# One attention unit's last products, kept keys and last queries rearranged in a fused attention and two-layer kernel

## Chip, cores and metric

The kernel runs on one core of a Trainium2 chip. Times are device microseconds of one launch. In the texts TensorE is PE in the rows, VectorE DVE, ScalarE ACT, GpSimd POOL, and SP the engine that issues the DMAs.

## What is computed

Sliding-window attention with a linear bias over 4 batches, 8 heads, 576 positions and 64 dimensions, followed by two feed-forward layers over the 2304 rows of 512:

```python
scores = scale * np.matmul(q, k.transpose(0, 1, 3, 2))
bias = slopes[:, None, None] * (-np.abs(rel).astype(np.float32))[None, :, :]
mask = (rel >= 0) & (rel < 128)
scores = np.where(mask, scores + bias[None], -1000000000.0)
...                                   # softmax over the keys
x = np.matmul(attn, v)                # then (tokens, 512)
h = np.maximum(x @ w_in, 0.0)
x = (h * h) @ w_out                   # 512 -> 2048 -> 512
x = 1 / (1 + np.exp(-(x @ w_gate))) * (x @ w_val) @ w_out2   # 512 -> 1536 -> 512
```

All is float32; the layers' operands are split into a high and a low part, three matmuls for each product.

## The kernel before

A query sees the 128 keys up to its own, so 128 queries need two key tiles of 128, their own and the one before. A **unit** is the attention of one batch for one pair of heads: kind a holds queries 0 to 255, kind b 256 to 511; kind c holds the last 64 queries of all four head pairs at once. Eight **chunks** of tokens are worked through in order: a and b of batch 0, a and b of batch 1 (four units each), then a with c of batch 0, b with c of batch 1, and so on (five units each). The first layer of a chunk (`h_step` and `y_step`, lines 795 to 861, 16 steps of each) runs while the units of the next chunk are worked on between its matmuls; the layers of chunks 0 and 1 are interleaved. The second layer (line 873 on) starts when all eight chunks are done.

A group of two head pairs is **turned** once (`turn`, line 558): queries (`nq`) and keys (`nk`) are loaded, transposed on TensorE (L584) into banks `tq` and `tk`, and copied by ScalarE to `qs` (L594, with a factor) and to `ka` or `ks` (L598). For kind c the queries are one tile of 64 rows and the 192 keys two of 96 rows, so that a group has six transposes.

A unit (`attend`, line 604) then goes through these steps: the **scores** (L638 for kind c, L653 for a and b) into two banks `ts`, a matmul for each head of the pair on one half of TensorE's rows; the float32 ones are two instructions each in the trace; the masks (L666) and the bias with the row minimum (L678) on VectorE; the exponential (L685) on ScalarE; the division (L699 on ScalarE or L701 on VectorE or GpSimd); transposes of the probabilities into `tp` (L741) and copies to `pt` (L745); selects of the window on GpSimd (L751); the **products** with the values into a bank `tv` (L778); and from it the high part of x on ScalarE (L338) and the low part on VectorE (L335).

For kind b the first 128 queries need the last key tile of kind a. The scores read it from `ka`, so that these queries' 256 keys are two matmuls of 128 columns for each head, one on `ka` and one on `ks`.

Nothing is issued in the order of the source. `op` records each step with the engines on which it may run, its planned cost, what it reads and writes, and a priority; `Plan.schedule` (line 117) plays the program through with these costs and gives one fixed order for each engine. Where several engines are allowed (`dve_or_pool`), it takes the one that is free first. Buffers have kinds with a highest number in use (`CAP`, and `CAP0` for the first three chunks), and a step whose buffer isn't free waits in that plan. The planned cost of a score step is a formula: 12 and 16 times `pe_ns(256)` = 109.1 ns for kinds a and b, and 16 times 82.5 + 100 ns for c.

Of the kernel before, what the change touches and what calls it, by code (L numbers as in the profile page):

```python
# [287 lines left out]
def attention_moe_moe2_kernel(ctx: ExitStack, tc, q, k, v, w_in, w_out1, w_gate, w_val, w_out2, out):  # L288
# [27 lines left out]
    CAP = {"raw": 3, "nq": 1, "nk": 1, "qs": 2, "ks": 2, "ka": 2, "wt": 6, "vs": 3, "st": 4, "pt": 2, "t": 3,  # L316
           "h": 2, "y": 4, "pg": 2, "pv": 2, "o": 6, "pa": 1, "pd": 1, "pa2": 1, "pd2": 1, "xacc": 2, "ob": 2, "ysg": 2, "raw2": 2, "pp": 2, "xp": 2,
           "tg": 2, "tw": 2, "st2": 5, "so": 5, "xf": 6, "cg": 4, "ss": 2, "ah": 12, "oc": 4, "qc": 3}
    CAP0 = {"nq": 3, "nk": 3, "qs": 2, "ks": 2, "ka": 3, "vs": 5, "st": 5, "pt": 6, "t": 6}
# [46 lines left out]
    C = {}  # L366
# [173 lines left out]
    X, TURNED, VT = {}, {}, {}  # L540
    FINE = 0

    def values(b, kind, chunk, prio):
# [7 lines left out]
        for h0, h1 in ((0, H // 2), (H // 2, H)) if chunk < FINE else ((0, H),):  # L551
            for t, vn in tiles.items():
                m = min(128, S - 128 * t)
                op({"SP": 250 + 60 * (h1 - h0)}, lambda e, vn=vn, t=t, m=m, h0=h0, h1=h1: nc.sync.dma_start(
                    out=vn()[0:m, h0:h1], in_=v[b, h0:h1, 128 * t:128 * t + m, :].rearrange("h p d -> p h d")),
                   w=[(vn, "v", h) for h in range(h0, h1)], prio=prio, data=182 / 2 * (h1 - h0) * m / 128)

    def turn(b, kind, g, chunk, p):

        early = chunk < 3  # L560
        nq, vq, vk = (2, 128, 128) if kind != "c" else (1, S - 512, (S - 384) // 2)
        a_q, a_k = {"a": (0, 0), "b": (256, 256), "c": (512, 384)}[kind]

        turns = ((0, 1), (1, 2)) if chunk < FINE else ((0, 2),)
        loaded = []
        for src, a, nt, r, name in ((q, a_q, nq, vq, "nq"), (k, a_k, 2, vk, "nk")):
            loaded.append((new(name, [128, nt, 4, 64], F32, early), src, a, nt, r))
        for i0, i1 in turns:
            for t, src, a, nt, r in loaded:
                op({"SP": 250 + 250 * (i1 - i0)}, lambda e, t=t, src=src, a=a, nt=nt, r=r, i0=i0, i1=i1: nc.sync.dma_start(  # L570
                    out=t()[0:r, :, 2 * i0:2 * i1], in_=src[b, 4 * g + 2 * i0:4 * g + 2 * i1, a:a + r * nt, :].rearrange("h (p j) d -> p j h d", j=nt)),
                   w=[(t, i) for i in range(i0, i1)], prio=p(0) - 3, data=2.85 * nt * r * (i1 - i0))

        qs = new("qs", [128, 2, nq * vq], F32, early)
        ks = new("ka" if kind == "a" else "ks", [128, 2, 2 * vk], F32, early)
        banks = [new("tq", [128, 512], F32, early)] * 2 if kind == "c" else [new(kd, [128, 512], F32, early) for kd in ("tq", "tk")]
        parts = ((qs, nq, vq, 0), (ks, 2, vk, 2 * vq if kind == "c" else 0))

        def flip(e, which, i0, i1):
            for z in which:  # L580
                _, nt, v_, c0 = parts[z]
                for i in range(i0, i1):
                    for j in range(nt):
                        nc.tensor.transpose(banks[z]()[:, c0 + (i * nt + j) * v_:c0 + (i * nt + j + 1) * v_],  # L584
                                            loaded[z][0]()[0:v_, j, 2 * i:2 * i + 2].rearrange("p h d -> p (h d)"), C["ident"][0:v_, 0:v_])

        c0 = parts[1][3]
        for i0, i1 in turns:
            for which in ((0, 1),) if kind == "c" else ((0,), (1,)):
                op({"PE": sum(parts[z][1] * 2 * (i1 - i0) * pe_ns(parts[z][2]) for z in which)}, lambda e, which=which, i0=i0, i1=i1: flip(e, which, i0, i1),  # L590
                   cols=.5, r=[(loaded[z][0], i) for z in which for i in range(i0, i1)], w=[(banks[z], z, i) for z in which for i in range(i0, i1)],
                   prio=p(1 + which[0] / 2), also=[parts[z][0] for z in which])
            for i in range(i0, i1):
                op({"ACT": act_ns(nq * vq, True) + 94}, lambda e, i=i: nc.scalar.activation(  # L594
                    out=qs()[:, i].rearrange("c (p j) -> c j p", j=nq),
                    in_=banks[0]()[:, i * nq * vq:(i + 1) * nq * vq].rearrange("c (j p) -> c j p", j=nq), func=AF.Copy,
                    scale=C["qmul"][:, 2 * g + i:2 * g + i + 1]), r=[(banks[0], 0, i)], w=[(qs, i)], prio=p(1.3))
            op({"ACT": act_ns(2 * vk * (i1 - i0), True)}, lambda e, i0=i0, i1=i1: nc.scalar.activation(  # L598
                out=ks()[:, i0:i1].rearrange("c i (p j) -> c i j p", j=2),
                in_=banks[1]()[:, c0 + 2 * vk * i0:c0 + 2 * vk * i1].rearrange("c (i j p) -> c i j p", i=i1 - i0, j=2), func=AF.Copy),  # L600
               r=[(banks[1], 1, i) for i in range(i0, i1)], w=[(ks, i) for i in range(i0, i1)], prio=p(1.8))
        TURNED[b, kind, g] = qs, ks

    def attend(u, due, long):
# [14 lines left out]
        vkeys = [(t_, "v", h) for t_ in vt.values() for hp in u.hps for h in (2 * hp, 2 * hp + 1)] + [(t_, "pad") for t_ in vt.values()]  # L619
# [4 lines left out]
        def plain(pr):  # L624
# [4 lines left out]
            kprev = TURNED[u.b, "a", groups[0]][1] if kind == "b" else None  # L629

            def go(e):
                if kind == "c":

                    for g, (qs, ks) in enumerate(turned):
                        for x in range(2):
                            for i in range(2):
                                rows = slice(64 * i, 64 * i + 64)
                                nc.tensor.matmul(both[g]()[rows, 256 * x:256 * x + S - 384], qs()[rows, x], ks()[rows, x], start=True, stop=True)  # L638
                    return
                qs, ks = turned[0]  # L640
                x = u.hps[0] % 2
                for j in range(nq):

                    if j > 0:
                        todo = [(ks, 0, 0, 256)]
                    elif kind == "b":
                        todo = [(kprev, 128, 0, 128), (ks, 0, 128, 128)]
                    else:
                        todo = [(ks, 0, 0, 128)]
                    for src, k0, c, w_ in todo:  # L650
                        for i in range(2):
                            rows = slice(64 * i, 64 * i + 64)
                            nc.tensor.matmul(both[i]()[:, 256 * j + c:256 * j + c + w_], qs()[rows, x, j * 128:(j + 1) * 128],  # L653
                                             src()[rows, x, k0:k0 + w_], start=True, stop=True)

            mine = sorted({hp % 2 for hp in u.hps})
            rd = [(k_, i) for t_ in turned for k_ in t_ for i in mine] + ([(kprev, i) for i in mine] if kind == "b" else [])
            op({"PE": {"a": 12 * pe_ns(256), "b": 16 * pe_ns(256), "c": 16 * pe_ns(S - 384) + 100}[kind]}, go, r=rd, w=both, prio=pr, also=[st, sm], cols=.5)
# [58 lines left out]
        N = 256  # L717
        cols = 64 if kind == "c" else 128
        if kind == "c":
            xpart = lambda z: x()[:, z, :, n0:n0 + 64]  # L720
        else:
# [560 lines left out]
```

## Time and profile before

| | us |
|---|---|
| median of 3 runs | 970.33 |
| lowest, highest | 968.18, 972.26 |
| profiled execution | 969.7 |
| its span, first to last instruction | 967.9 |

| engine | busy us | share of the span |
|---|---|---|
| TensorE, matmuls | 950.9 | 98% |
| VectorE | 622.3 | 64% |
| ScalarE | 566.3 | 59% |
| GpSimd | 192.0 | 20% |

The mean granted clock of TensorE is 0.994 of full speed. Busy times of matmuls overlap, as they are pipelined, and their ends are modelled; what a matmul costs is seen in the chain of waits, where each piece goes from one end to the next.

### The profile page before, as it was taken

To read this page: it belongs to the slowest core of one execution; us is meant where nothing else is said; L and a number is where in the kernel's file an instruction comes from. 1 tells how busy PE (TensorE), PEld (TensorE's weight loads), DVE (VectorE), ACT (ScalarE), POOL (GpSimd) and SP (SyncE) were. 2 spreads that over 40 slices of the span, in tenths; PEclk is the share of its full clock that TensorE was granted. 3 is DMA by queue.
4 is the path that set the end of the run, shared out by engine and by line. 5 is a ranking of instruction groups with operands and counts; after the bars stand their busy time and mean duration, and the time that the engine had idled before them with its cause. 6 is when DMAs were issued, how large, how long until landed. Compare 5 with 4: busy or idle time off the path is not lost.

```text
span 967.9 us, 21379 instructions
## 1 busy us (share of the span) xinstructions
PE 950.9 (98%) x7728; PEld 913.6 (94%) x7728; DVE 622.3 (64%) x1608; ACT 566.3 (59%) x1496; POOL 192.0 (20%) x277
## 2 busy tenths in 40 slices
PE   8899999999999999999999999999999999999997
PEld 6589999989999998999999999999999999999997
DVE  7999986777676687677552133645765585476555
ACT  6988777668677677576654422544544544454442
POOL 3611112223224112112200000102211230222001
PEclk9989999999999999999999999999999999999999
DMA  9765446584664873963599941566776687678931
GB/s 229 174 178 163 151 121 206 175 264 160 193 206 158 230 213 133 264 209 136 158 348 376 385 143 34 189 215 225 252 254 210 214 279 223 212 241 264 348 113 45
DMA packets 181929, 200.64 MB, mean 207 GB/s; under 512 B 80192, under 2 KB 113472, under 8 KB 181824
## 3 DMA queue, kind: packets, MB, share of 16 engines
q1 hardware_dynamic: 181824, 199.27, 65.1%
q8 instruction: 62, 1.02, 0.4%
q14 instruction: 43, 0.35, 0.1%
HBM read 152.04 MB, written 47.19 MB: 206 GB/s over the span
## 4 chain that ended last, share of the span: by engine, by line
PE 91%; ACT 3%; DMA 2%; DVE 2%; POOL 1%; SPq 1%; issue 0%; POOLq 0%; DVEq 0%; ACTq 0%
PE y L841 21%; PE pa L962 14%; PE pd L962 11%; PE o L1120 10%; PE h L804 7%; PE h L805 7%; PE h L806 7%; PE tv L778 3%; PE ts L653 2%; PE o L1087 2%; PE pd L1120 2%; PE tp L741 1%; PE tq L584 1%; ACT st L685 1%; DMA nq<-in_q_dram 1%; DMA wscr<-pp 1%
## 5 line engine op out<-in xcount | busy, mean ns | idle before, releaser
L841 PE MATMUL y<-gs,wh 128*128 128x256 f32 (+1 forms) x1024 | 216.0, 303 | 3.7 <-DVE gs L335 2.8
L841 PEld LDWEIGHTS y<-gs,wh 128*128 128x128 f32 x1024 | 165.1, 191 | 10.3 <-issue 4.8
L804 PE MATMUL h<-x,wh 128*128 128x256 f32 (+1 forms) x512 | 155.0, 303 | 0.6 <-ACT pt L745 0.6
L841 PE MATMUL y<-gs,wl 128*128 128x256 f32 (+1 forms) x512 | 152.2, 297 | 0.0
L805 PE MATMUL h<-x,wh 128*128 128x256 f32 (+1 forms) x512 | 151.2, 295 | 0.0
L806 PE MATMUL h<-x,wl 128*128 128x256 f32 (+1 forms) x512 | 151.1, 295 | 0.0
L338 ACT ACTIVATE cg<-pa 128x256 f32<-128x256 f32 x144 | 54.8, 382 | 109.4 <-PE pa L962 105.9
L335 DVE TENSOR_TENSOR gs<-r,gs 128x320 fp32r<-128x320 f32 (+1 forms) x115 | 54.7, 475 | 72.1 <-ACT gs L338 71.6
L804 PEld LDWEIGHTS h<-x,wh 128*128 128x128 f32 x512 | 96.7, 189 | 4.2 <-issue 1.9
L841 PEld LDWEIGHTS y<-gs,wl 128*128 128x128 f32 x512 | 97.7, 191 | 0.0
L818 ACT ACTIVATE r<-h 128x256 f32<-128x256 f32 (+1 forms) x128 | 51.9, 406 | 76.8 <-PE h L806 76.3
L805 PEld LDWEIGHTS h<-x,wh 128*128 128x128 f32 x512 | 96.7, 189 | 0.0
L806 PEld LDWEIGHTS h<-x,wl 128*128 128x128 f32 x512 | 96.6, 189 | 0.0
L962 PE MATMUL pa<-x,st 128*128 128x256 f32 x576 | 84.2, 282 | 0.0
L751 POOL TENSOR_SCALAR_AFFINE_SELECT pt<-pt 128x256 f32<-128x256 f32 (+1 forms) x120 | 62.8, 549 | 106.5 <-ACT pt L745 105.5
L978 DVE TENSOR_TENSOR cg<-cg,pd 128x256 f32<-128x256 f32 x96 | 40.4, 421 | 61.0 <-PE pd L962 59.7
L962 PEld LDWEIGHTS pa<-x,st 128*128 128x128 f32 x576 | 75.1, 189 | 0.0
L1120 PE MATMUL o<-wr,ah 128*128 128x256 f32 x432 | 70.4, 281 | 0.2 <-DVE ah L335 0.2
L1120 PE MATMUL o<-so,ah 128*128 128x256 f32 x432 | 66.3, 281 | 0.0
L685 ACT ACTIVATE st<-st,sm 128x128 f32<-128x128 f32 x144 | 56.4, 397 | 10.7 <-DVE sm L678 10.7
L338 ACT ACTIVATE gs<-r 128x256 fp32r<-128x256 f32 (+1 forms) x128 | 56.6, 442 | 9.1 <-PE y L841 2.6
L1120 PEld LDWEIGHTS o<-wr,ah 128*128 128x128 f32 x432 | 59.5, 189 | 0.4 <-DVE ah L335 0.4
(179 smaller groups left out, 2050.4 us busy)
## 6 DMA issues: line engine op xcount, KB each, us to landing
st<-wscr SPq DMA_DIRECT2D x192, 256.0 KB, 3.4
wscr<-pp SPq DMA_DIRECT2D x72, 512.0 KB, 3.4
so<-wscr SPq DMA_DIRECT2D x96, 256.0 KB, 3.5
raw<-in_moe_w_out_dram SPq DMA_DIRECT2D x28, 512.0 KB, 3.8
wr<-wscr SPq DMA_DIRECT2D x54, 256.0 KB, 5.4
raw<-in_moe_w_in_dram SPq DMA_DIRECT2D x16, 512.0 KB, 4.7
vs<-in_v_dram SPq DMA_DIRECT2D x24, 256.0 KB, 5.1
raw<-in_moe_w_gate_dram SPq DMA_DIRECT2D x12, 512.0 KB, 4.3
```

What stands on the lines that cost most here:

```text
L335: return lambda e: eng(e).tensor_tensor(out=out(), in0=a(), in1=b(), op=ALU.subtract)
L338: return lambda e: nc.scalar.activation(out=out(), in_=in_(), func=AF.Copy, scale=scale)
L685: op({"ACT": 386}, lambda e, x=x: nc.scalar.activation(out=st()[:, x, :], in_=st()[:, x, :], func=AF.Exp, bias=sm()[:, x:x + 1], scale=-1. ...
L751: op({"POOL": pool_sel(512 // nq)}, lambda e: nc.gpsimd.affine_select(out=pt_of(what, j), in_=pt_of("own", j), pattern=[[0, 512 // (nq * c ...
L804: nc.tensor.matmul(ps()[:, :N], w[0]()[:, c], x()[:, 0, cc, :N], start=cc == 0, stop=False)
L805: nc.tensor.matmul(ps()[:, :N], w[0]()[:, c], x()[:, 1, cc, :N], start=False, stop=False)
L806: nc.tensor.matmul(ps()[:, :N], w[1]()[:, c], x()[:, 0, cc, :N], start=False, stop=cc == CC - 1)
L818: op({"ACT": act_ns(N, True)}, lambda e: nc.scalar.activation(out=g()[:, :N], in_=ps()[:, :N], func=AF.Relu), r=[ps], w=[g], prio=ep, also ...
L841: nc.tensor.matmul(y()[:, c0:c0 + N], w[a]()[:, c], gs()[:, b, :N], start=f == 0 and p == 0 and n != 1, stop=f == F1 - 1 and p == 2, skip_ ...
L962: nc.tensor.matmul(ps()[:, :256], w()[:, z * 256 + cc * 128:z * 256 + cc * 128 + 128], x, start=start and cc == 0 and i == 0, stop=cc == 1 ...
L978: op({"DVE": dve_ns(256)} if psum else dve_or_pool(256), lambda e: eng(e).tensor_tensor(out=quarter(i, j)(), in0=quarter(i, j)(), in1=src( ...
L1120: nc.tensor.matmul(o()[:, 256 * t:256 * t + 256], a_()[:, c_ + 128 * t:c_ + 128 * t + 128], w()[:, 256 * z:256 * z + 256], start=start and ...
```

## The change

Four things are done.

- From chunk 3 on, two units of kind a or b write their products into one bank `tv`, the second's behind the first's in one step. One ScalarE copy and one VectorE subtraction of 512 columns follow for both. `pt` may be held four times.
- For kind b, `ks` becomes one tile of 384 columns for each head pair: 128 kept keys, copied from `ka` by ScalarE or GpSimd, and the 256 new ones. The first 128 queries' scores are one matmul of 256 columns for each head. `ks` may be held three times, four in the first chunks.
- For kind c, all heads of a batch are loaded at once: one tile holds the 64 queries above their own 64 keys, another the 128 keys before them. Each group has four 128x128 transposes into one bank and two copies of keys.
- The planned cost of a score step is a number: 1056 ns for a and b, 1643 for c.

```diff
-    CAP = {..., "ks": 2, ..., "pt": 2, "t": 3,
+    CAP = {..., "ks": 3, ..., "pt": 4, "t": 3,
-    CAP0 = {"nq": 3, "nk": 3, "qs": 2, "ks": 2, ...}
+    CAP0 = {"nq": 3, "nk": 3, "qs": 2, "ks": 4, ...}
...
-    FINE = 0
+    MERGE = 3
...
     def turn(b, kind, g, chunk, p):
...
+            ks = [new("ka", [128, 2, 256], F32, early)] if kind == "a" else [new("ks", [128, 384], F32, early) for _ in range(2)]
...
+                else:
+                    for i in range(2):
+                        op({"ACT": act_ns(256, True)}, lambda e, i=i, bank=bank: nc.scalar.activation(
+                            out=ks[i]()[:, 128:384].rearrange("c (p j) -> c j p", j=2),
+                            in_=bank()[:, 256 * i:256 * i + 256].rearrange("c (j p) -> c j p", j=2), func=AF.Copy), r=[bank], w=[(ks[i], 1)], prio=p(1.8))
...
+            for i in range(2):
+                def carry(e, i=i):
+                    if e == "ACT":
+                        nc.scalar.activation(out=ks[i]()[:, 0:128], in_=before[i]()[:, 128:256], func=AF.Copy)
+                    else:
+                        nc.gpsimd.tensor_copy(ks[i]()[:, 0:128], before[i]()[:, 128:256])
+
+                op({"ACT": act_ns(128), "POOL": pool_ns(128)}, carry, r=keys[i], w=[(ks[i], 0)], prio=p(1.8))
...
+        if g == 0:
+            own, prev = LAST[b] = new("nq", [128, H, 64], F32, early), new("nk", [128, H, 64], F32, early)
+            for t, src, r0, a0, n in ((own, q, 0, 512, S - 512), (own, k, S - 512, 512, S - 512), (prev, k, 0, 384, 128)):
+                op({"SP": 750}, lambda e, t=t, src=src, r0=r0, a0=a0, n=n: nc.sync.dma_start(
+                    out=t()[r0:r0 + n], in_=src[b, :, a0:a0 + n, :].rearrange("h p d -> p h d")), w=[(t, r0)], prio=p(0) - 3, data=5.7 * 2 * n)
+        own, prev = LAST[b]
...
+            for z, t in enumerate((own, prev)):
+                for i in range(2):
+                    nc.tensor.transpose(bank()[:, 256 * z + 128 * i:256 * z + 128 * i + 128],
+                                        t()[:, 4 * g + 2 * i:4 * g + 2 * i + 2].rearrange("p h d -> p (h d)"), C["ident"])
...
-                    if j > 0:
-                        todo = [(ks, 0, 0, 256)]
-                    elif kind == "b":
-                        todo = [(kprev, 128, 0, 128), (ks, 0, 128, 128)]
-                    else:
-                        todo = [(ks, 0, 0, 128)]
...
+                    k0, w_ = (128 * j, 256) if kind == "b" else (0, 128 + 128 * j)
+                    for i in range(2):
+                        rows = slice(64 * i, 64 * i + 64)
+                        nc.tensor.matmul(both[i]()[:, 256 * j:256 * j + w_], qs()[rows, x, j * 128:(j + 1) * 128],
+                                         ks[x]()[rows, k0:k0 + w_], start=True, stop=True)
...
-            op({"PE": {"a": 12 * pe_ns(256), "b": 16 * pe_ns(256), "c": 16 * pe_ns(S - 384) + 100}[kind]}, go, ...)
+            op({"PE": {"a": 1056, "b": 1056, "c": 1643}[kind]}, go, r=rd, w=both, prio=pr, also=[st, sm], cols=.5)
...
+        PROBS[u.b, kind, u.hps[0]] = mid, ends
+        both = kind != "c" and u.chunk >= MERGE
+        if both and u.hps[0] % 2 == 0:
+            return
         vp = new("tv", [128, 512], F32, early)
...
+        hps = [u.hps[0] - 1, u.hps[0]] if both else u.hps
+        for y, hp in enumerate(hps):
...
+            m_, e_ = PROBS.pop((u.b, kind, hp))
+            ks_ += [(m_, 0), (m_, 1), (e_, 0), (e_, 1)]
+            c = 256 * y
+            prods.append((u.q0, 2 * hp, lambda i, m_=m_: m_()[:, i].rearrange("p j c -> p (j c)"), c, c + 256, True, False))
...
+        N = 512 if both else 256
+        vpart = lambda: vp()[:, :N].rearrange("p (c t) -> p c t", c=len(hps))
+        xpart = lambda z: x()[:, z, hps[0]:hps[-1] + 1, n0:n0 + N // len(hps)]
```

## Rows read from the trace of the kernel before

**Rows 1.** Stretches: us busy (instructions) of each engine, granted clock, DMA share, GB/s.

```profile
0.00:25.00 25.00, 20.33 (x144) 17.65 (x144) 17.77 (x79) 16.49 (x51) 8.82 (x36) 0.93 1.01 229
25.00:50.00 25.00, 20.74 (x181) 14.91 (x180) 23.27 (x104) 24.68 (x95) 14.92 (x28) 0.96 0.65 162
50.00:75.00 25.00, 23.93 (x180) 21.67 (x180) 24.48 (x75) 20.00 (x60) 5.74 (x9) 0.91 0.64 190
75.00:100.00 25.00, 25.00 (x214) 24.54 (x213) 23.58 (x50) 19.22 (x50) 2.54 (x4) 1.00 0.51 159
...
575.00:600.00 25.00, 25.00 (x212) 25.00 (x211) 4.81 (x13) 4.90 (x12) 0.00 (x0) 1.00 0.13 43
```

In each line the engines are PE, PEld (weight loads), DVE, ACT and POOL.

**Rows 2.** TensorE's waits: total us, times, longest us.

```profile
PE y L841 <- DVE gs L335: 2.8, 1, 2.8
...
PE y L841 <- ACT gs L338: 0.8, 1, 0.8
```

**Rows 3.** Chain of waits around two product groups: start us, us, what.

```profile
143.82 1.45 PE tv L778 x16
145.27 0.32 PE h L804
145.59 0.12 PE h L805
...
146.18 0.80 PE tv L778 x8
146.98 0.56 PE y L841 x3
```

**Rows 4.** Chain of waits, a product group behind a score group of kind b.

```profile
187.69 1.08 PE ts L653 x12
188.77 1.02 PE tv L778 x12
189.79 0.55 PE y L841 x3
```

**Rows 5.** Chain of waits at kind c's transposes and scores, and at four full transposes.

```profile
251.77 0.75 PE tq L584 x6
...
253.96 1.45 PE ts L638 x16
...
267.99 0.44 PE tq L584 x4
268.43 0.71 PE y L841 x6
```

**Rows 6.** Chain of waits, a score group of kind a.

```profile
232.84 0.86 PE ts L653 x8
```

**Rows 7.** Chain of waits before TensorE's longest wait, and a little later.

```profile
36.57 0.51 ACT ka L598
37.08 0.26 ACT pt L745
...
37.40 5.79 POOL pt L751 x9
...
48.28 0.34 DVE gs L335
...
57.43 1.16 ACT st L699 x4
```

**Rows 8.** Stretches right behind that wait, columns as in the first group.

```profile
49.00:51.50 2.50, 2.50 (x13) 2.50 (x13) 2.50 (x7) 1.25 (x3) 0.00 (x0) 0.50 0.19 43
51.50:54.00 2.50, 2.50 (x14) 2.50 (x13) 2.27 (x7) 1.73 (x4) 0.00 (x0) 0.50 0.91 275
```

**Rows 9.** Groups by form, GpSimd: its only plain copies of float32.

```profile
L397 POOL COPY relc<-rel 64x128 f32<-64x128 f32 x2 | 0.6, 288 | 0.1
```

**Rows 10.** Timeline: the last low part of x for chunk 3, its first L804.

```profile
204.36 0.42 DVE L335 TENSOR_TENSOR x<-tv,x 128x256 fp32r<-128x256 f32 x1
...
209.93 0.28 PE L804 MATMUL h<-x,wh 128*128 128x256 f32 x1
```

More of the change, by code (lines that the diff above doesn't have):

```diff
@@ L550, in values @@
                 op({"POOL": 150 + 2.1 * 512}, lambda e, vn=vn, m=m: nc.gpsimd.memset(vn()[m:128], 0.0), w=[(vn, "pad")], prio=prio)
-        for h0, h1 in ((0, H // 2), (H // 2, H)) if chunk < FINE else ((0, H),):
+        for h0, h1 in ((0, H),):
             for t, vn in tiles.items():
@@ L556, in values @@
                    w=[(vn, "v", h) for h in range(h0, h1)], prio=prio, data=182 / 2 * (h1 - h0) * m / 128)
+    LAST = {}
     def turn(b, kind, g, chunk, p):
         early = chunk < 3
[L561 to L601, printed above, removed]
@@ new lines, in turn, with flip @@
+        m = S - 512
+        qs, ks, bank = new("qs", [128, 2, m], F32, early), new("ks", [128, 2, 128 + m], F32, early), new("tq", [128, 512], F32, early)
+        def flip(e):
+            for z, t in enumerate((own, prev)):
+                for i in range(2):
+                    nc.tensor.transpose(bank()[:, 256 * z + 128 * i:256 * z + 128 * i + 128],
+                                        t()[:, 4 * g + 2 * i:4 * g + 2 * i + 2].rearrange("p h d -> p (h d)"), C["ident"])
+        op({"PE": 436}, flip, cols=.5, r=[(own, 0), (own, m), (prev, 0)], w=[bank], prio=p(1), also=[qs, ks])
@@ new lines, in turn @@
+        for i in range(2):
+            op({"ACT": act_ns(m, True) + 94}, lambda e, i=i: nc.scalar.activation(
+                out=qs()[:, i], in_=bank()[:, 128 * i:128 * i + m], func=AF.Copy, scale=C["qmul"][:, 2 * g + i:2 * g + i + 1]),
+               r=[bank], w=[(qs, i)], prio=p(1.3))
+        for z, (c0, c1) in enumerate(((128, 128 + m), (0, 128))):
+            op({"ACT": act_ns(2 * (c1 - c0), True)}, lambda e, z=z, c0=c0, c1=c1: nc.scalar.activation(
+                out=ks()[:, :, c0:c1], in_=bank().rearrange("c (z i p) -> c z i p", z=2, i=2)[:, z, :, (128 - m if z == 0 else 0):], func=AF.Copy),
+               r=[bank], w=[(ks, z)], prio=p(1.8))
@@ L604, in attend @@
+        TURNED[b, kind, g] = qs, [(lambda i=i: ks()[:, i]) for i in range(2)], [[(ks, 0), (ks, 1)]] * 2
     def attend(u, due, long):
@@ L628, in plain @@
             turned = [TURNED[u.b, kind, g] for g in groups]
-            kprev = TURNED[u.b, "a", groups[0]][1] if kind == "b" else None
             def go(e):
                 if kind == "c":
-                    for g, (qs, ks) in enumerate(turned):
+                    for g, (qs, ks, _) in enumerate(turned):
                         for x in range(2):
@@ L716, in attend @@
         n0 = 256 * u.part
-        N = 256
         cols = 64 if kind == "c" else 128
-        if kind == "c":
-            xpart = lambda z: x()[:, z, :, n0:n0 + 64]
-        else:
-            xpart = lambda z: x()[:, z, u.hps[0], n0:n0 + 256]
-        xout = lambda z: [(x, z, hp, u.part) for hp in u.hps]
         shape = [128, 2, 2, 128] if kind != "c" else [128, 2 * HP, 1, 64]
@@ L779, in go @@
                                      start=start, stop=stop, skip_group_check=True)
+        vkeys = [(t_, "v", h) for t_ in vt.values() for hp in hps for h in (2 * hp, 2 * hp + 1)] + [(t_, "pad") for t_ in vt.values()]
         op({"PE": sum(4 * pe_ns(pr_[4] - pr_[3]) + 46 for pr_ in prods) + 54}, go, cols=.5, r=vkeys + ks_,
            w=[vp], prio=p(9), also=[x])
[L783 to L786 removed]
+        N = 512 if both else 256
+        vpart = lambda: vp()[:, :N].rearrange("p (c t) -> p c t", c=len(hps))
+        xpart = lambda z: x()[:, z, hps[0]:hps[-1] + 1, n0:n0 + N // len(hps)]
+        xout = lambda z: [(x, z, hp, u.part) for hp in hps]
         op({"ACT": act_ns(N, True)}, copy(lambda: xpart(0), vpart), r=[vp], w=xout(0), prio=p(10))
```

72 lines of the change are left out of this document (45 added, 27 removed).

## The prediction, made before the changed kernel ran

> **What bounds the kernel now.** I read the stretches of the span first, then TensorE's waits, then the chain of waits at the places that the change touches. [rows 1] show two regimes. From 75 us on TensorE is busy for all of nearly every 25 us stretch at a granted clock of 1.00 (75 to 100 stands for these, 575 to 600 shows that the second layer is the same). In the first 75 us it is not: there ScalarE is busy 24.68 of 25 us between 25 and 50, VectorE 23.27, and TensorE has holes. [rows 2] say the same from the other side: the longest wait of TensorE, 2.8 us, is in that beginning, and after it there is one of 0.8 us. So after 75 us every nanosecond taken out of TensorE's queue comes off the end, and work taken from VectorE or ScalarE is worth nothing; before 75 us it is nearly the other way round.
>
> What a short group costs TensorE is read from the chain, whose pieces go from one matmul's end to the next. A matmul of the first layer with 256 columns costs 0.12 us. Around a product group (L778) it doesn't stay so: the L804 behind it takes 0.32, and three of L841 take 0.56 in place of 0.36 [rows 3]. This array-shape change costs 0.20 us outside the group. Inside it there is more: two first-kind units whose products happen to lie next to each other are 16 instructions in 1.45 us, one alone is 8 in 0.80, so 0.15 us of the second group goes when it follows directly [rows 3]. A product group that joins another saves 0.15 + 0.20 = 0.35 us; one that already stands behind a score group (L653, then L778, then 0.56 for three L841 [rows 4]) has had the 0.20 already, and saves 0.15.
>
> **The change, part by part.**
>
> *Two units' products in one bank.* From chunk 3 on (chunks 3 to 7, four units of kind a or b in each) 20 product groups become 10. Columns and matmuls stay as they are. Bounds: 10 x 0.15 = 1.5 us and 10 x 0.35 = 3.5 us. Five of the 20 groups stand behind a score group now, the one of [rows 4] and four like it, so I take 10 x (0.35 - 0.20 x 5/20) = 3.0 us. The evacuations fall from 20 copies of 256 columns to 10 of 512 on ScalarE, and the subtractions on VectorE likewise; behind a TensorE that never waits that is worth nothing. The first unit of a pair now gets its x later: its product, with all matmuls behind it in TensorE's queue, waits for the second unit's selects on GpSimd. The tightest place is chunk 3: the last x is ready at 204.36 + 0.42 = 204.78 and the chunk's first L804 runs at 209.93 [rows 10], 5.1 us later. I cost this at nothing; if that slack were gone, each microsecond of a late last product would be one of the end.
>
> *The last 64 queries.* Each of 8 groups turns six pieces of 64 and 96 rows in 0.75 us; four full 128x128 transposes are 0.44 us [rows 5], and with no cost behind them. Saving 8 x 0.31 = 2.5 us. The loads become three for a batch in place of four, with the same bytes, issued by SP before the first group's turn; two tiles are then held over both groups. The key copy becomes two instructions on ScalarE, outside the bound. The scores keep 16 instructions of 192 columns, 1.45 us [rows 5]: nothing there.
>
> *The kept key tile.* A second-kind (b) unit's scores go from 12 instructions (8 of 128 columns, 4 of 256) to 8 of 256. A kind a unit has 4 of 128 and 4 of 256 and takes 0.86 us [rows 6]; b takes 1.08 [rows 4], so four of 128 columns cost 0.22, or 0.055 each. If 256 columns cost twice that, the fixed part of a group is 0.86 - 0.22 - 0.44 = 0.20, and the new group is 8 x 0.11 + 0.20 = 1.08: no gain. Bounds for the 16 units: with L804's 0.12 for each instruction 1.16, a loss of 16 x 0.08 = 1.3 us; with the group as cheap as a's 0.86 a gain of 16 x 0.22 = 3.5 us. I take nothing, since 0.055 for 128 and 0.11 to 0.12 for 256 columns are the nearest rows and are proportional to the columns. The Trainium skill (TensorE: Matmul & The Clock Gate, Back-to-back issue gap) would have it otherwise: it gives about 81 ns for a sustained matmul of 128 columns and 131 ns for 512, so that fewer, wider ones are cheaper for each column; by an estimate from it, 98 ns at 256, the 12 instructions take 1.04 us, the 8 take 0.78, and the 16 units gain 4.1 us. The trace has 55 ns where the page has 81, so it doesn't agree.
>
> The copies themselves are 16 of 128 columns, on ScalarE or GpSimd, whichever is free first: like L699, of which four in a row take 1.16 us in the chain [rows 7], or like GpSimd's 0.29 us for half the partitions [rows 9]. The new key copies are two of 256 columns for one of 512: in the chain 0.26 for 256 and 0.51 for 512 [rows 7], so nothing. Twelve of the 16 copies lie in chunks 3, 5 and 7, where TensorE hides them. Four lie in chunk 1, in the stretch in which ScalarE is full: at worst 1.2 us, all on ScalarE, at best nothing, as GpSimd has about 10 of its 25 us free there [rows 1]. I take 0.3 us.
>
> *Capacities and planned score times.* These add no instruction. They change the order that is worked out for every engine, since the planner's times for a score group fall from 1.31 and 1.75 us to 1.06, and rise from 1.42 to 1.64 for the last queries. After 75 us, where other engines run ahead, I cost that at nothing. In the beginning it can go either way: TensorE stands idle there for 2.84 us, because VectorE serves masks, weights and x first and the subtraction for the waiting L841 last, after a run of nine GpSimd selects that takes 5.79 us [rows 7]; and the clock is at 0.50, its lower level of 1.2 GHz, from 49 to 54 us, right behind that wait [rows 8], 5 us at half speed, so 2.5 us lost.
>
> **The sum.** The profiled execution took 969.7 us: a span of 967.9 and 1.8 around it. -3.0 - 2.5 + 0 + 0.3 = -5.2, so 964.5. That execution was 0.6 under the median of 970.33; against the median I expect **965.1**, 0.54% less.
>
> **The rivals.**
> - *A better beginning.* The new order serves the waiting L841 earlier: the 2.84 us wait goes, and with it the 2.5 us lost to the clock. 965.1 - 5.3 = 959.8. For it: planned times nearer to those of [rows 4] and [rows 6]. Against: VectorE is busy 24.48 of 25 us from 50 to 75 too [rows 1], so that a wait removed in one place can come back in another.
> - *A worse beginning.* A copy of the kept keys for chunk 1 falls into GpSimd's queue behind a run of selects like the nine of [rows 7]; the score group waits for it, and all of TensorE's queue behind that. Price 5.79 us, and 2.5 us at the lower clock behind it: 8.3. 965.1 + 8.3 = 973.4, slower than before; if both groups of that chunk meet it, 981.7. It decides from 5.2 us of added wait on. Against: the kept tile is turned long before, so the copy can run as soon as its buffer is there.
> - *Half of the gain.* The products stood next to other short groups more often than I count, or now come to stand alone (1.5 us), all four early copies land on ScalarE (1.2 us): -1.5 - 2.5 + 1.2 = -2.8, so 967.5.
> - *Scores in a's time.* The new b group takes 0.86 us: 3.5 us more, 961.6. The planner's new figure, the same for a and b, says so; the rows say columns. By the rule of the Trainium skill above (TensorE: Matmul & The Clock Gate, Back-to-back issue gap) it would be an estimated 4.1 us.
>
> **How the numbers follow.** A measurement of this kernel can tell about 0.5% from no change, 4.9 us: below 965.5 is faster, above 975.2 slower. Chances: the forecast 0.47 (its own range 963 to 967, just over half of it below 965.5), a better beginning 0.15, a worse one 0.14 (half of it above 975.2), half the gain 0.19, scores in a's time 0.05. Faster: 0.26 + 0.15 + 0.05 + 0.04 = 0.50; slower 0.07, taken as 0.08; within the bound 0.42. The range reaches from the better beginning to one worse one, 959.5 to 973.5.
>
> **What would show it.** In the profile after: product groups of 16 or 24 instructions from chunk 3 on, 10 of them, each followed by one slow L804 or L841; transposes of the last queries at 0.44 us in fours; b scores 8 instructions in about 1.08 us; TensorE still without waits between 75 and 560 us; 16 copies of 128 columns on ScalarE and GpSimd. TensorE's matmul time after 75 us should fall by some 5 us. The prediction is wrong if the first 75 us end more than 2 us earlier or later in their work, if a wait over 1 us comes up after 75 us, or if the b scores take 0.86.

## The result and the profile after

The changed kernel takes **960.54 us** (median of 4 runs, 959.63 to 962.53) against 971.30 for the kernel before beside it: a ratio of 0.9904 (95% interval 0.9881 to 0.9928; this is the ratio on record, as below, and the two medians alone would give 0.9889). A second series (e5) gave 959.44 against 969.67, 0.9897 (0.9881 to 0.9913). The profiled execution took 959.64, its span 957.9, 10.1 us less than the one before. So it is faster, by 1.8 to 1.9 times the forecast's 0.54%.

| engine | busy us before | after |
|---|---|---|
| TensorE, matmuls | 950.9 | 941.2 |
| VectorE | 622.3 | 631.2 |
| ScalarE | 566.3 | 560.9 |
| GpSimd | 192.0 | 186.8 |

After the change the lines are: first layer L833 to L835 and L870 (L804 to L806 and L841 before), products L806, scores L679 (a and b) and L670 (c), transposes L580 (a and b) and L624 (c), second layer from L991, its first matmul L1087 (L1058 before). `warm` (L1266, L1237 before) are matmuls whose result nobody uses: the planner puts them into TensorE's order at moments in which its plan of the first 21 us has that engine idle.

The stretches of the changed kernel, columns as in [rows 1]:

```profile
0.00:25.00 25.00, 20.63 (x154) 16.88 (x156) 18.39 (x89) 17.82 (x61) 8.45 (x39) 1.00 1.08 227
25.00:50.00 25.00, 20.54 (x176) 15.74 (x172) 24.21 (x88) 23.45 (x85) 14.45 (x26) 1.00 0.71 164
50.00:75.00 25.00, 23.62 (x196) 22.09 (x197) 24.56 (x80) 22.16 (x66) 5.25 (x6) 1.00 0.61 177
```

The granted clock in the first three, 0.93, 0.96 and 0.91 in [rows 1], is 1.00 in all. VectorE and ScalarE are as full as before. TensorE's waits of the changed kernel, to be read against [rows 2]:

```profile
PE tq L580 <- DMA nq<-in_q_dram: 2.9, 2, 1.7
PE warm L1266 <- DVE identr L382: 1.8, 1, 1.8
PE tk L580 <- DMA nk<-in_k_dram: 1.3, 1, 1.3
PE ts L679 <- DVE x L335: 1.3, 1, 1.3
PE y L870 <- DVE gs L335: 1.1, 1, 1.1
```

The wait of 2.84 us is 1.1 now, but others have come: all of TensorE's waits in the first 100 us add up to 10.3 us, before to 10.0. What went is not waiting but the low clock behind it. Small stretches of the kernel before, around two places where its clock fell, and of the changed kernel at the first of them:

```profile
12.50:15.00 2.50, 0.86 (x5) 0.86 (x5) 2.47 (x21) 2.05 (x11) 0.61 (x1) 0.75 1.17 211
15.00:17.50 2.50, 2.50 (x16) 2.50 (x14) 2.08 (x6) 1.61 (x6) 0.72 (x1) 0.57 1.01 237
...
50.00:52.50 2.50, 2.50 (x14) 2.50 (x14) 2.50 (x7) 0.47 (x2) 0.00 (x0) 0.50 0.45 149
52.50:55.00 2.50, 2.50 (x15) 2.27 (x16) 2.27 (x7) 2.22 (x5) 0.00 (x0) 0.56 0.95 251
```

```profile
12.50:15.00 2.50, 1.28 (x11) 1.29 (x12) 2.47 (x18) 2.40 (x12) 1.33 (x2) 1.00 1.35 218
15.00:17.50 2.50, 2.22 (x20) 1.66 (x18) 2.50 (x6) 1.89 (x6) 0.35 (x1) 1.00 1.18 255
```

I estimate the time lost to the clock as 25 us times what each stretch lacks to 1.00: 25 x (0.07 + 0.04 + 0.09) = **5.0 us** before, 0 after. Below I call this the lost clock.

The chain of waits of the changed kernel, at the parts that were edited (start us, us, what), against [rows 3 to 6]:

```profile
171.26 1.89 PE tv L806 x24
173.15 0.91 PE y L870 x6
...
181.67 1.06 PE ts L679 x8
...
219.34 0.86 PE ts L679 x8
220.20 0.55 PE y L870 x3
220.75 1.45 PE tv L806 x16
222.20 0.32 PE h L833
...
237.08 0.44 PE tq L624 x4
...
243.55 1.45 PE ts L670 x16
```

Two product groups of kind b are now 24 instructions in 1.89 us (twice 1.02 before), two of kind a 16 in 1.45 (twice 0.80), and the 0.20 us of the array-shape change follows once. The b scores take 1.06 us (1.08 before), a's 0.86 as before. The last queries' transposes take 0.44 (0.75 before), their scores 1.45 as before. The copies of the kept keys, groups by form (busy us, mean ns; idle before):

```profile
L604 ACT ACTIVATE ks<-ka 128x128 f32<-128x128 f32 x13 | 3.7, 301 | 0.0
...
L606 POOL COPY ks<-ka 128x128 f32<-128x128 f32 x3 | 1.4, 464 | 20.7 <-PE ts L670 15.5 <-ACT ka L589 5.2
```

**Where the 10 us went.** Each chunk has 64 instructions of L804 (L833 after), so a chunk's first one, and the second layer's first matmul, can be found in both traces (us from the start of the span):

| | chunk 2 | chunk 4 | second layer | end of span |
|---|---|---|---|---|
| before | 155.5 | 274.9 | 548.9 | 967.9 |
| after | 149.6 | 267.8 | 538.5 | 957.9 |
| difference | -5.9 | -7.1 | -10.4 | -10.0 |

5.9 us are gained before chunk 2, where nothing is merged and no last query is turned; 4.5 between there and the second layer; the second layer itself takes 419.4 in place of 419.0. All of this is from one execution of each, and a chunk's first matmul is a mark that moves with the order, by up to 3.6 us: e8 and e9 below have the same order of TensorE up to 92 us and begin chunk 4 at 267.5 and 267.2, but chunk 2 at 152.0 and 148.4.

### The profile page after: what moved, and what is told of

Its sections match the earlier page's. It is cut to its first block, busy times and chain, and to the rows that moved or that the text cites. A ratio compares the mean times of both kernels' runs of the same rounds, so it can differ in the third digit from the quotient of the medians.

```text
span 957.9 us, 21191 instructions
## 1 busy us (share of the span) xinstructions
PE 941.2 (98%) x7650; PEld 908.1 (95%) x7650; DVE 631.2 (66%) x1622; ACT 560.9 (59%) x1496; POOL 186.8 (20%) x271
## 4 chain that ended last, share of the span: by engine, by line
PE 89%; DVE 5%; DMA 2%; ACT 2%; SPq 1%; issue 1%; POOLq 0%; DVEq 0%
PE y L870 20%; PE pa L991 14%; PE pd L991 11%; PE o L1149 10%; PE h L833 7%; PE h L835 6%; PE h L834 6%; PE tv L806 3%; PE ts L679 2%; PE o L1116 2%; PE pd L1149 2%; DMA raw<-in_moe_w_in_dram 1%; PE tp L761 1%; DVE wt L432 1%; ACT st L711 1%
## 5 line engine op out<-in xcount | busy, mean ns | idle before, releaser
L870 PE MATMUL y<-gs,wh 128*128 128x256 f32 (+1 forms) x1024 | 214.3, 301 | 1.1 <-DVE gs L335 1.1
L870 PEld LDWEIGHTS y<-gs,wh 128*128 128x128 f32 x1024 | 163.5, 189 | 8.2 <-issue 3.8
L833 PE MATMUL h<-x,wh 128*128 128x256 f32 (+1 forms) x512 | 154.3, 301 | 0.3 <-ACT r L847 0.3
L870 PE MATMUL y<-gs,wl 128*128 128x256 f32 (+1 forms) x512 | 151.4, 296 | 0.3 <-DVE wl L335 0.3
L835 PE MATMUL h<-x,wl 128*128 128x256 f32 (+1 forms) x512 | 151.3, 295 | 0.0
L335 DVE TENSOR_TENSOR gs<-r,gs 128x256 fp32r<-128x256 f32 (+1 forms) x122 | 58.0, 476 | 63.9 <-ACT gs L338 63.5
L833 PEld LDWEIGHTS h<-x,wh 128*128 128x128 f32 x512 | 96.6, 189 | 3.0 <-issue 1.0
L870 PEld LDWEIGHTS y<-gs,wl 128*128 128x128 f32 x512 | 96.6, 189 | 0.5 <-DVE wl L335 0.5
L835 PEld LDWEIGHTS h<-x,wl 128*128 128x128 f32 x512 | 96.5, 189 | 0.0
L771 POOL TENSOR_SCALAR_AFFINE_SELECT pt<-pt 128x256 f32<-128x256 f32 (+1 forms) x120 | 60.7, 532 | 135.6 <-ACT pt L765 134.6
L991 PE MATMUL pa<-x,st 128*128 128x256 f32 x576 | 84.3, 282 | 0.0
L991 PEld LDWEIGHTS pa<-x,st 128*128 128x128 f32 x576 | 75.2, 189 | 0.0
```

Source lines behind the costliest of these rows:

```text
L335: return lambda e: eng(e).tensor_tensor(out=out(), in0=a(), in1=b(), op=ALU.subtract)
L771: op({"POOL": pool_sel(512 // nq)}, lambda e: nc.gpsimd.affine_select(out=pt_of(what, j), in_=pt_of("own", j), pattern=[[0, 512 // (nq * c ...
L833: nc.tensor.matmul(ps()[:, :N], w[0]()[:, c], x()[:, 0, cc, :N], start=cc == 0, stop=False)
L835: nc.tensor.matmul(ps()[:, :N], w[1]()[:, c], x()[:, 0, cc, :N], start=False, stop=cc == CC - 1)
L870: nc.tensor.matmul(y()[:, c0:c0 + N], w[a]()[:, c], gs()[:, b, :N], start=f == 0 and p == 0 and n != 1, stop=f == F1 - 1 and p == 2, skip_ ...
L991: nc.tensor.matmul(ps()[:, :256], w()[:, z * 256 + cc * 128:z * 256 + cc * 128 + 128], x, start=start and cc == 0 and i == 0, stop=cc == 1 ...
```

## The experiments

Theory A, held first: the edits' own terms are as predicted, and the rest is the planned times, which are nearer to the truth and so order the beginning better. Rival: some edit does it directly.

### One part at a time: e1 to e4

Each is the kernel before with one part of the diff above and the capacities that this part needs; e2 to e4 keep the old planned times. e1:

```diff
-            op({"PE": {"a": 12 * pe_ns(256), "b": 16 * pe_ns(256), "c": 16 * pe_ns(S - 384) + 100}[kind]}, go, ...)
+            op({"PE": {"a": 1056, "b": 1056, "c": 1643}[kind]}, go, ...)
```

> The kernel before with one edit: the planned cost of a score step is 1056, 1056 and 1643 ns. No instruction is added or removed, only orders change, from the 11th line of TensorE's order on. Theory A (the beginning is shorter in the changed kernel because the planned score times are nearer to the truth): chunk 2 starts at about 149.6 us in place of 155.5, the 2.8 us wait for a VectorE subtraction near 46 us and the half clock behind it are gone, and the time is 5 to 6 us shorter than before. Theory B (the kept keys and their buffers changed the beginning): no gain here, chunk 2 starts at 155 +- 1 us. Theory C (any new order moves the beginning by some microseconds, either way): a start of chunk 2 that fits neither. After chunk 2 nothing changes: 393 us to the second layer, +- 1.

e2:

```diff
-    CAP = {..., "pt": 2, ...}
+    CAP = {..., "pt": 4, ...}
+    MERGE = 3
...
+        both = kind != "c" and u.chunk >= MERGE
+        if both and u.hps[0] % 2 == 0:
+            return
```

> The kernel before with only the products of two units in one bank (from chunk 3 on, pt held up to four times). TensorE's order is the same as before for its first 831 lines, so that the beginning is not touched under any theory: chunk 2 starts at 155.5 +- 1 us. By my term 10 groups fewer save 3.0 us, bounds 1.5 and 3.5, all of it between chunk 3 and the second layer. If the 0.20 us behind a group is not paid by TensorE at all, the gain is at the lower end, 1.5 us.

e3:

```diff
+        if kind == "c":
+            if g == 0:
+                own, prev = LAST[b] = new("nq", [128, H, 64], F32, early), new("nk", [128, H, 64], F32, early)
...
+            op({"PE": 436}, flip, cols=.5, r=[(own, 0), (own, m), (prev, 0)], w=[bank], prio=p(1), also=[qs, ks])
```

> The kernel before with only the last 64 queries turned above their own keys. TensorE's order is the same as before for its first 1185 lines. By my term 8 groups of transposes save 0.31 us each, 2.5 us, between chunk 4 and the second layer; the beginning stays at 155.5 +- 1 us. If the trace's longer groups were only overlapped time, the gain is under 1 us.

e4:

```diff
-    CAP = {..., "ks": 2, ...}
+    CAP = {..., "ks": 3, ...}
-    CAP0 = {..., "ks": 2, ...}
+    CAP0 = {..., "ks": 4, ...}
...
+                op({"ACT": act_ns(128), "POOL": pool_ns(128)}, carry, r=keys[i], w=[(ks[i], 0)], prio=p(1.8))
...
+                    k0, w_ = (128 * j, 256) if kind == "b" else (0, 128 + 128 * j)
```

> The kernel before with only the kept key tile copied next to the new ones (ks held up to three times, four in the first chunks), products and last queries as before, planned score times as before. By my term the scores gain nothing in themselves (0 +- 0.3 us after chunk 2). The order of the beginning changes from the 6th line of TensorE on. Theory A: the beginning gets no shorter, or longer by up to 1.2 us from four copies. Theory B: the beginning is shorter by about 6 us, chunk 2 starts near 150 us. Theory C: some other start of chunk 2.

| | us | before | ratio, 95% interval | effect us |
|---|---|---|---|---|
| e1, times | 966.57 | 969.58 | 0.9971 (0.9962 to 0.9980) | -2.8 |
| e2, products | 965.95 | 969.58 | 0.9966 (0.9953 to 0.9979) | -3.3 |
| e3, last queries | 965.90 | 969.58 | 0.9970 (0.9960 to 0.9980) | -2.9 |
| e4, kept keys | 967.15 | 969.58 | 0.9979 (0.9970 to 0.9988) | -2.0 |

The effects (1 minus the ratio, times 969.6) add up to -11.0, the whole change to -10.0 beside e5. By the medians alone they are 3.0, 3.6, 3.7 and 2.4, 12.7 in all, against 10.2 for e5. With intervals of about 1 us either way that is near, but e1 and e4 order the same beginning anew, and nothing shows that two such gains add; there it may be chance. e5's -10.0 lies between the 8.5 to 9.5 and the 11.0 of its expectation below.

In e1 chunk 2 begins at 153.5, neither at the 149.6 of its theory A nor at the 155 of B: the new times alone give less than half of the changed kernel's gain there. e2 and e3 keep TensorE's order of the beginning and its lost clock (5.25 and 5.0 us): theirs is pure saving behind it, near the size that was predicted. e4 has its gain elsewhere: chunk 2 begins at 153.0 in place of 155.5, which is again neither A nor B, and from there to the second layer it takes 393.7 us against 393.4 before. The scores give nothing; the beginning does, whose lost clock is 3.5 in place of 5.0:

```profile
0.00:25.00 25.00, 20.75 (x141) 18.07 (x141) 17.69 (x79) 16.71 (x54) 8.85 (x36) 0.93 1.10 229
25.00:50.00 25.00, 21.81 (x181) 16.12 (x181) 23.73 (x96) 23.12 (x88) 15.33 (x28) 1.00 0.67 176
50.00:75.00 25.00, 22.81 (x184) 21.59 (x181) 24.31 (x75) 20.47 (x62) 4.65 (x6) 0.93 0.49 151
```

### Are true planned times what helps? e5 to e8

e5 is the changed kernel again, without an edit.

> The changed kernel again, beside the kernel before on one chip, for a narrower interval. If the four parts add up (2.8 + 3.3 + 2.9 + 2.0 us by the medians of the four kernels with one part each), it is 11.0 us shorter than before, ratio 0.9887; if the two parts that reorder the beginning share one gain, it is 8.5 to 9.5 us shorter, ratio 0.990 to 0.991.

e6 is the changed kernel with the old planned times:

```diff
-            op({"PE": {"a": 1056, "b": 1056, "c": 1643}[kind]}, go, ...)
+            op({"PE": {"a": 12 * pe_ns(256), "b": 16 * pe_ns(256), "c": 16 * pe_ns(S - 384) + 100}[kind]}, go, ...)
```

> The changed kernel with the old planned score times (12 and 16 times 109.1 ns, and 16 times 82.5 + 100). Theory A (nearer planned times make the beginning shorter): 2.5 to 3 us slower than the changed kernel, all of it before chunk 2. Theory C (any new order moves the beginning): any other difference, a gain too. If the kept keys and the times share one gain, under 1 us.

e7 and e8 are the kernel before with other numbers. e7:

```diff
-            op({"PE": {"a": 12 * pe_ns(256), "b": 16 * pe_ns(256), "c": 16 * pe_ns(S - 384) + 100}[kind]}, go, ...)
+            op({"PE": {"a": 1056, "b": 1279, "c": 1643}[kind]}, go, ...)
```

> The kernel before with planned score times of 1056, 1279 and 1643 ns: those which its own trace shows (0.86, 1.08 and 1.45 us and the 0.20 behind a group). Theory A: at least the gain of 1056, 1056, 1643, so 2.8 us or more below before, as the figure for kind b is nearer. Theory C: it differs from that kernel by more than 1 us in either direction.

e8, in the same place:

```diff
+            op({"PE": {"a": 700, "b": 700, "c": 1100}[kind]}, go, ...)
```

> The kernel before with planned score times of 700, 700 and 1100 ns, too low by about as much as the old ones of kinds a and b are too high. Theory A: no gain over before, or slower. Theory C, or a rule that smaller planned times are better whatever the truth: a gain as large as with 1056, 1056, 1643, 2 to 4 us.

| | us | before | ratio, 95% interval |
|---|---|---|---|
| e5, changed kernel | 959.44 | 969.67 | 0.9897 (0.9881 to 0.9913) |
| e6, its old times | 962.76 | 969.67 | 0.9933 (0.9915 to 0.9952) |
| e7, b at 1279 | 969.76 | 969.67 | 1.0003 (0.9993 to 1.0013) |
| e8, 700 and 1100 | 964.77 | 969.67 | 0.9954 (0.9938 to 0.9970) |

In the changed kernel the planned times are worth 0.36%, 3.5 us (2.8 in e1): with the old ones (e6) 1.75 us of lost clock are back in the first 25 us. But **theory A falls.** The groups take 0.86, 1.08 and 1.45 us in the chain. e7's numbers are all some 0.2 above that, nearer than the old ones for a and b, and give nothing; e8's are further off than e7's for b and c, by 0.38 and 0.35 too low, and give 4.5 us. e7 loses less clock than before, 1.75 us, but its waits in the first 100 us add up to 12.7 us in place of 10.0, and the two nearly cancel. Its stretches, and the wait of its beginning behind which its clock fell (timeline; in brackets the idle time before):

```profile
0.00:25.00 25.00, 19.91 (x156) 16.52 (x156) 18.52 (x89) 16.75 (x54) 7.27 (x36) 1.00 1.00 226
25.00:50.00 25.00, 21.45 (x175) 16.21 (x172) 23.80 (x89) 22.94 (x82) 14.69 (x25) 0.93 0.66 164
```

```profile
42.68 0.39 PE L841 MATMUL y<-gs,wh 128*128 128x256 f32 x1 [2.18 <-DVE gs L335]
```

e5 holds a control that was not planned. It is the same program as the profiled changed kernel, in the same order, but in this execution a DMA came later. The timeline of the first profile, then of e5:

```profile
32.30 0.63 PE L580 MATMUL tk<-identr,nk 128*128 128x128 f32 x4 [1.35 <-DMA nk<-in_k_dram]
32.86 1.14 PE L679 MATMUL ts<-ks,qs 64*128 64x256 f32 x8
...
34.34 0.37 PE L833 MATMUL h<-x,wh 128*128 128x256 f32 x1
```

```profile
32.59 1.09 PE L580 MATMUL tk<-identr,nk 128*128 128x128 f32 x4 [1.77 <-DMA nk<-in_k_dram]
33.61 2.08 PE L679 MATMUL ts<-ks,qs 64*128 64x256 f32 x8
...
36.17 0.37 PE L833 MATMUL h<-x,wh 128*128 128x256 f32 x1
```

and e5's stretch there:

```profile
32.50:35.00 2.50, 2.41 (x10) 1.90 (x12) 1.69 (x9) 2.27 (x6) 0.61 (x1) 0.51 1.27 274
```

A wait 0.42 us longer, the clock at its lower level of 1.2 GHz behind it (0.51 in the stretch), the eight score matmuls 2.08 us in place of 1.14: the first layer begins 1.83 us later, and the span is 959.3 in place of 957.9. In this pair the lost clock is thus a cost by itself, not a sign of some other.

### The order of the beginning: e9 and e10

Theory B: it is the order of the first chunks that the times change, and only in them do they matter. Theory D: it takes no better times, any small change tips the order.

Both are the kernel before. e9, with e8's numbers in chunks 0 to 2 only:

```diff
+            op({"PE": {"a": 700, "b": 700, "c": 1100}[kind] if early else {"a": 12 * pe_ns(256), "b": 16 * pe_ns(256), "c": 16 * pe_ns(S - 384) + 100}[kind]}, go, ...)
```

> The kernel before with the low planned score times (700, 700, 1100 ns) only for the units of the first three chunks, the old formula from chunk 3 on; no instruction added or removed. Theory B (the gain of falsely low times lies in the order of the beginning, where TensorE waits for VectorE and loses its clock): most of the 4.7 us that low times gave everywhere comes back, 4 to 5 us less than the kernel before (ratio 0.995 to 0.996), first L804 of chunk 4 at about 269 instead of 274.9 us, and the rest from there unchanged at 278 or so to the end of the first layer. Rival C (the low times order the units of the later chunks better as well): under 2.5 us here, the rest missing between chunk 3 and the second layer.

e10, the old times 3% lower:

```diff
+            op({"PE": .97 * {"a": 12 * pe_ns(256), "b": 16 * pe_ns(256), "c": 16 * pe_ns(S - 384) + 100}[kind]}, go, ...)
```

> The kernel before with its own planned score times times 0.97, nothing else. If the order of the beginning is settled by ties that any small change tips (theory D), the time moves by 1 us or more either way (ratio outside 0.999 to 1.001) although the times stay as wrong as before, and TensorE's longest wait in the first 75 us, 2.8 us on L841, has another size or place. If only a change in one direction, towards shorter scores, helps (theory B with a size), 0 to 1 us less, since times 19% lower for a and b gave 2.8 us. If neither, 0 within 0.3 us and the same order.

e9: 962.94 against 969.43, 0.9932 (0.9919 to 0.9944), -6.6 us. e10: 965.20 against 969.43, 0.9952 (0.9938 to 0.9965), **-4.7 us by nothing but a 3% change of planned numbers.** e9's gain is larger than the 4 to 5 us that theory B had named. Both have no lost clock. In e9 chunk 4 begins at 267.2, and from there to the second layer it takes 274.5 us, as the kernel before with 274.0 (to the last matmul of the first layer, which the expectation's 278 counts to, it is 277.9 and 277.3). e10's stretches and its longest waits:

```profile
0.00:25.00 25.00, 20.00 (x159) 16.62 (x161) 18.98 (x86) 18.25 (x58) 9.55 (x38) 1.00 1.09 228
25.00:50.00 25.00, 20.34 (x182) 15.71 (x179) 22.34 (x97) 22.98 (x84) 14.32 (x27) 1.00 0.68 178
50.00:75.00 25.00, 23.65 (x204) 22.50 (x205) 23.95 (x75) 21.44 (x67) 5.56 (x8) 1.00 0.49 143
```

```profile
PE tq L584 <- DMA nq<-in_q_dram: 2.0, 1, 2.0
PE warm L1237 <- DVE identr L382: 1.8, 1, 1.8
PE tp L741 <- DVE sm L693: 1.6, 1, 1.6
PE tv L778 <- DVE sm L678: 1.4, 1, 1.4
```

TensorE waits more in e10 than before, 10.9 us in the first 100 in place of 10.0, but in smaller pieces, and its clock stays at its upper level, 2.4 GHz. e9 waits less as well. All kernels that differ from the one before in planned numbers alone can be put on one scale: the change of lost clock plus the change of waits in the first 100 us, beside the moment at which chunk 4 begins (274.9 before). The column `warm` is explained below the table.

| | lost clock | waits | expected by both | chunk 4 | warm |
|---|---|---|---|---|---|
| e1 | 3.5 | 10.2 | -1.3 | -2.8 | 8 |
| e7 | 1.75 | 12.7 | -0.6 | -1.0 | 8 |
| e10 | 0 | 10.9 | -4.1 | -4.4 | 7 |
| e8 | 0 | 7.3 | -7.7 | -7.5 | 12 |
| e9 | 0 | 6.9 | -8.1 | -7.8 | 12 |

Within 1.5 us the two columns agree. Theories B and D hold together: the gain of the beginning is clock and waits, and what sets them is which plan the numbers fall into. e8 begins as e9 does but loses 1.9 us between chunk 4 and the second layer, in the order of its later units.

A rival for part of this stands untested: a plan is not only an order. It also sets how many warming matmuls run right before TensorE's DMA wait at 14 us, the column `warm`; the kernel before has 6. (So "no instruction is added or removed" in the expectations of e1 and e9 holds for the kernel's own work alone: e9 has 55 warming matmuls in all, the kernel before 48.) In all five profiled executions with 6 of them, the kernel before, e2, e3, e4 and e6, the clock fell at that wait, for 1.75 us lost in the first 25 us. In the nine with 7 or more it fell there once, in e1, 1.5 us behind the wait. Up to that wait e10 has the instructions of the kernel before and one warming matmul more. No run changed this number alone, so 1.75 us of the 5.0 may be owed to it and not to the order; the other 3.25 us were lost 30 us later, behind the wait for `gs`.

### Can the changed kernel be helped further? e11 and e12

Both are the changed kernel. e11 with e8's numbers everywhere, e12 with them in chunks 0 to 2:

```diff
-            op({"PE": {"a": 1056, "b": 1056, "c": 1643}[kind]}, go, ...)
+            op({"PE": {"a": 700, "b": 700, "c": 1100}[kind]}, go, ...)
```

> The changed kernel with planned score times of 700, 700, 1100 ns in place of 1056, 1056, 1643. If low times give the beginning what they gave in the kernel before (4.7 us against 2.8 us for the changed kernel's own times), another 2 us: 957.5 to 958.5, ratio 0.9877. If the changed kernel's beginning is already without waits (granted clock 1.00 in all of the first 75 us), nothing is left to gain: 959 to 960.5, ratio 0.9895, or worse by what another order costs, up to the 3.5 us that its old times cost.

```diff
+            op({"PE": ({"a": 700, "b": 700, "c": 1100} if early else {"a": 1056, "b": 1056, "c": 1643})[kind]}, go, ...)
```

> The changed kernel with planned score times of 700, 700, 1100 ns for the first three chunks alone, its own 1056, 1056, 1643 from chunk 3 on. TensorE's order in the second layer is again that of the changed kernel, row for row, and its order in the beginning that of the kernel with low times everywhere. If the 8.6 us that low times everywhere cost there came from the order of the second layer, they are gone: the second layer takes 419.4 us again, and the first L806 to L833 work of chunk 2 begins 2 us earlier than in the changed kernel: 957.5 to 958.5 us, ratio 0.9870 to 0.9885. If they came from something else in the later units, it stays above 963. If the low times were good for the beginning only together with the later ones, 959 to 961 us as the changed kernel itself.

e11: 967.20 against 969.43, 0.9977 (0.9967 to 0.9987): 7 to 8 us worse than the changed kernel, more than any theory had. Its second layer begins 1.0 us earlier (537.5), but takes 428.0 us in place of 419.4. TensorE's waits in it from 580 us on, and two stretches (matmuls in brackets; the changed kernel has 419 and 423 there):

```profile
PE pd L991 <- DVE cg L1007: 2.2, 3, 1.2
PE pd L991 <- DVE xacc L1167: 1.2, 1, 1.2
PE pa L991 <- DVE cg L1036: 0.8, 1, 0.8
```

```profile
600.00:650.00 50.00, 48.72 (x405) 48.00 (x404) 28.05 (x58) 22.37 (x53) 9.92 (x9) 1.00 0.65 213
650.00:700.00 50.00, 48.44 (x402) 47.67 (x402) 33.09 (x58) 24.02 (x56) 16.76 (x16) 1.00 0.73 238
```

No score runs there: the planned times had changed the order of the second layer, most of the waits being for VectorE's `cg`. e12 has the changed kernel's order there, and 418.8 us; it takes 958.83 against 969.59, 0.9891 (0.9875 to 0.9908). So the order cost the 8.6 us. The trace lists only 5 to 6 us of idle time for TensorE there, but idle time counts short: a matmul of 256 columns lasts 0.28 us in the trace, while in an unbroken run the next begins 0.12 us after it. Counted from one matmul's start to the next, e11's second layer has 37 steps of over 0.2 us, 14.9 us in all, the changed kernel's 8 with 2.2 us; 29 steps of 0.12 us, 3.5 us, taken off, that is 9.2 us, somewhat more than the whole loss. In the beginning e12 gains little on the changed kernel, which had no lost clock any more: chunk 4 begins at 267.5 in place of 267.8, though its waits are 8.5 in place of 10.3, and chunk 2 begins at 151.7, 2.1 us later and not 2 us earlier as expected. It is not to be told from the changed kernel, whose interval its own overlaps.

## Why the prediction was right in direction and short in size

965.1 was forecast, in a range of 959.5 to 973.5; 960.54 was measured, near its lower end. By steps:

- **Merged products: right.** -3.0 predicted, -3.3 measured alone. Ten groups, 0.15 us less in each and one slow follower in place of two, as the rows said. The evacuations cost nothing, and TensorE's one wait between 75 us and the second layer is 0.3 us: that the first unit of a pair gets its x later did not matter.
- **Last queries: right.** -2.5 predicted, -2.9 measured alone; 0.75 became 0.44 in the chain.
- **Kept keys' scores: right, nothing.** 1.06 us measured for 1.08 predicted. The rule of the Trainium skill (TensorE: Matmul & The Clock Gate, Back-to-back issue gap), under which the 16 units would have gained an estimated 4.1 us, does not show: 1.08 became 1.06, 0.3 us for 16 units.
- **Early copies: not separable.** 13 of the 16 copies went to ScalarE and 3 to GpSimd; what the four early ones cost is buried in e4's better beginning. The +0.3 can't be confirmed, and was not what mattered.
- **Planned times and capacities: wrong.** They stood at nothing, with a rival of 0.15 for a better beginning. This is the step that failed, and its own test, a beginning over 2 us earlier, shows it: chunk 2 begins 5.9 earlier. Measured alone, the times give 2.8 us and e4's new order 2.0, together nearly the part that the forecast lacks: 3.0 + 2.5 - 0.3 = 5.2 forecast, 3.3 + 2.9 + 2.0 + 2.8 = 11.0 by parts.

The rival of a better beginning named 959.8, and it is the one that came, but its working was only half right. It priced the 2.84 us wait and 2.5 us of half clock behind it. The wait did go, but others took its place (10.0 and 10.3 us in sum), as the argument against that rival had it. The clock was worth twice as much: [rows 1] already had 0.93 in the first 25 us, 1.75 us lost behind the DMA wait at 14 us, which I left out, and 3.25 us from 25 to 75 us, of which I priced 2.5. 5.0 us could have been read there.

By the mark of chunk 2 the changed kernel gains 5.9, where lost clock and waits give 5.0 - 0.3 = 4.7; but that mark moves with the order. By the mark of chunk 4 the account closes: e2 begins it 2.3 us earlier than the kernel before and e3 0.2, with the 4.7 that is 7.2 for the 7.1 measured. From there to the second layer e2 saves 1.9 and e3 1.6, 3.5 for 3.3 measured. The same sum is 2.2 us too large for e6 and 1.6 for e12, so it is good to about 2 us and no better.

The chance for such a beginning was too small for another reason. I weighed whether the new planned times were better; e10 shows that a change need not be better to help. The plan of the kernel before was probably a poor one: each of e1, e4, e8, e9 and e10 has less lost clock and a gain (e8's and e9's beginnings are nearly one), and only e7, with more waits, gains nothing. e11 shows the other side: a new order can as well cost 8.6 us, in a layer that the edit does not touch.

## What to carry to other kernels

Where a planner writes out the order, an edit is two changes, its own saving and a new draw of the order: measure the second by itself, with the planned numbers moved a few per cent and the kernel's own work left alone, before the first is credited with it; and see what else the plan sets, here the number of warming matmuls. Read the granted clock of every early stretch and add up what each lacks to 1.00; that sum is an estimate of a gain in reach, and it did not go with the sum of TensorE's waits. Savings of short groups in a queue that never waits were priced from the chain to 0.3 and 0.4 us here, inside the intervals of e2 and e3.

## What the hardware showed

Whether the clock falls behind a wait is not told by the wait's length alone. Behind a DMA wait of 2.30 us at 14 us it fell in the kernel before, and the same nine warming matmuls took 2.27 us, 1.31 in the changed kernel. The timeline of the kernel before, then of the changed one:

```profile
10.86 0.97 PE L1237 MATMUL warm<-identr 128*128 128x256 f32 x6
14.14 1.11 PE L584 MATMUL tq<-identr,nq 128*128 128x128 f32 x4 [2.30 <-DMA nq<-in_q_dram]
14.90 2.27 PE L1237 MATMUL warm<-identr 128*128 128x256 f32 x9
```

```profile
10.68 1.34 PE L1266 MATMUL warm<-identr 128*128 128x256 f32 x9
13.71 0.66 PE L580 MATMUL tq<-identr,nq 128*128 128x128 f32 x4 [1.70 <-DMA nq<-in_q_dram]
14.13 1.31 PE L1266 MATMUL warm<-identr 128*128 128x256 f32 x9
```

But e7 had a DMA wait of 2.31 us there and kept 1.00 in its first 25 us:

```profile
10.77 1.22 PE L1237 MATMUL warm<-identr 128*128 128x256 f32 x8
14.30 0.66 PE L584 MATMUL tq<-identr,nq 128*128 128x128 f32 x4 [2.31 <-DMA nq<-in_q_dram]
14.71 1.31 PE L1237 MATMUL warm<-identr 128*128 128x256 f32 x9
```

Behind 1.8 us at this place it fell in e6, behind 2.0 in e10 it did not. What goes with it in these rows is the work ahead of the wait: 6 warming matmuls in the kernel before and in e6, 7 in e10, 8 in e7, 9 in the changed kernel. That is what the rows show and no test of it; e1 lost the clock 1.5 us after this wait with 8.

The same program, too, loses it in one execution and not in another: e5 lost it behind 1.77 us at 32 us, the first profile of the changed kernel kept it behind 1.35. The first four runs of the changed kernel have mean granted clocks of 0.998, 0.998, 0.997 and 0.995 and take 959.64, 959.63, 961.44 and 962.53 us, and 0.003 of 960 us is the 2.9 us between the first and the last. It is not always so close: in the 60 runs of the kernel before that stand beside e1 to e12, a mean clock lower by 0.001, 1 us at that price, goes with 0.5 us more. The lost clock as it is estimated here may thus be more than it costs.
